# Batch 0's folds on one engine, its first DFT stage framed by zero products, its tables loaded sooner, and the order planned anew

## The chip, the cores and the metric

One core of a Trainium2 chip runs the whole program. The metric is device time in microseconds (us), the median of three runs. TensorE (PE) multiplies matrices into PSUM; VectorE (DVE) and ScalarE (ACT) work on tiles in SBUF and PSUM; GpSimd (POOL) works on SBUF and issues the indirect loads; the queue of SyncE (SP) issues all other transfers, in order. Each engine runs its own instructions in program order, and semaphores hold one engine for another.

## The reference

Eight batches of 576 tokens. Attention has 8 heads of 64 (four with a local mask of 32 tokens, four strided by 32); its output is x, 576 by 512 per batch. Then comes a mixing block: the real part of a two-dimensional Fourier transform is added to x, the sum is normalised, and two dense layers with a ReLU between them are added on top.

```python
scores = np.where(masks[None], scale * np.matmul(q, k.transpose(0, 1, 3, 2)), -1e9)
attn = softmax(scores);  x = heads_joined(np.matmul(attn, v))        # (8, 576, 512)
mixed = np.real(np.fft.fft(np.fft.fft(x, axis=1), axis=2))
u = x + mixed
un = (u - mean(u)) / np.sqrt(var(u) + 1e-6)
out = u + np.maximum(un @ w_ch1, 0.0) @ w_ch2                        # 512 -> 2048 -> 512
```

## The kernel before, in words

The work is cut into attention pairs (two heads of a batch, four pairs per batch), a Fourier transform per batch, and 18 chunks of 256 tokens for the dense layers. A chunk's first layer is its eight "ups" (line 1387, 24 matmuls each), its second layer its "downs" (line 1427). Almost all of TensorE's time goes there: W1 and W2 come as 64-bit words, are put together on ACT and DVE (lines 1215 to 1237) and split into two float16 halves (lines 1303 to 1306 for W1, 1339 to 1344 for W2), and each product takes three float16 passes. No up can run before batch 0 is through its transform and its normalisation, and no down before the halves of W2 that it reads are written.

Nothing is placed by hand. Each step is a generator that yields an `op` with an engine, an assumed duration, rooms that it takes and gives back, events that it needs, and, for some, an `alt`: a second engine with an added cost. A planner (`Order.run`) takes the ready step with the earliest start by its own clock, and among steps of that engine within a small window the one with the lowest bias. The biases, windows and added costs stand in the dictionary `P`; the program's order on every engine follows from them. While a Gram bank is open, the planner fills idle stretches of TensorE with products of zeros (`rest`, line 1272), as many as its own clock says will fit.

Batch 0 goes first, in this chain. The four pairs write their output to DRAM (lines 845 to 859). `fft_load` reads it back as `xa` in one plain load and four indirect gathers by POOL (line 897), of tokens n and 576-n. The step E adds the two, O subtracts them. Then the channels are folded, all at line 907: `cosb` and `cosd` add mirrored halves of E, `cosf` folds once more into FD, `cos2` fills FD's third group; `sin` and `sin2` do the same with O. `side(c0, c1)` forms the sums and differences of a group's two token halves: columns 0 to 129 (`side 0`) and 129 to 257 from E, 257 to 512 (`side 257`) from O. In batch 0 the planner had put E, the folds and `cos2` on DVE, and O and all three sides on POOL.

`products32` is batch 0's transform in float32. Its first stage, A, has five column groups of 65, 64, 128, 127 and 128 (0 and 1 read side 0, 2 reads side 129, 3 and 4 read side 257). A group is one product over the 33 last tokens (line 1060, 290 columns, from FD) and two over 128 tokens (line 1063, 145 columns each, from the sides); the trace shows each float32 product as two records. The tables for it, `f32a` and `f32b` (435 and 528.5 KB), are issued at line 390, and `late` makes them wait until the gathers of batch 0 have landed. ACT or DVE copies A's groups out (line 1072), then stage B multiplies by the second table (lines 1083 to 1095). B opens and closes each bank with a bf16 product of zeros:

```python
T.matmul(ps[:, 0:512], zerb, zero.to_broadcast([128, 512]), start=True, stop=False)
...
T.matmul(ps[:, 0:512], zerb, zero.to_broadcast([128, 512]), start=False, stop=True)
```

`sums` adds x (line 1099), `norm` normalises (lines 1155 to 1181), and the turned halves `uT` open the first up. Batches 3 to 7 use a float16 form of the same transform (lines 907 to 1038) with the same step names.

Of the kernel before, what the change touches and what calls it, by code (L numbers as in the profile page):

```python
# [21 lines left out]
P = dict(  # L22
    SL2=2.667, SLD2=1.764, GL0=2.7, GD=7.0, LAT=2.22, GL=3.1, t2=47.947, l0=-31.68, a0=-20, sq0=-23.456, w0a=-19.97,
    c=12.731, z=13.906, f0=-24.028, w0=-22.847, s0=-1.359, w1=3.314, s1=-5.983, p0=-26.912, p1=4.962, pn=-4.352,
    a1=-14.294, f1=-1.92, a2=0.121, f2=8.514, an=8.61, fn=-44.611, db=1.982, up=19.467, dn=25.786, ev=0.684, WS=0.271,
    WV=0.084, WA=0.048, WG=0.877, WT=0.185, SL=0.0, SLD=0.818, np=3, AL=3.136, SG=2.918, Lcl=-0.367, Lsg=0.875, LQ=0,
    LO0=12.439, LE0=13.019, Lc20=-1.501, LSD0=-13.8, al=0.0, Lfs=-1.909, Lwl=-2.741, Lul=-9.275, LO=24.795, LE=5.158,
    Lc2=-1.062, LSD=-13.902, Lsub=1.259, Lsub0=28.179, Lrt=14.582, Lu=5.511, ORD0=(3, 2, 0, 1),
    vo=([], [], [], [0, 1, 2, 3]), S0=('qk', 'qk', 'kt', 'pt'),
    S1=('uT', 'kt', 'f6', 'uT', 'kt', 'uT', 'f6', 'f6', 'kt', 'pt', 'uT', 'qk', 'u', 'f6', 'kt', 'qk'), M1=(), HB=4,  # L30
    RB=1, UB=8, VS=1, FC=15, tp=-0.006, ts=0.377, fq=-18.063, fh=-13.401, ff=-23.53, pf=5.385, Lfold=79.934, Lus=0.177,
    Lhl=1.519,
# [7 lines left out]
UB = P["UB"]  # L40
# [261 lines left out]
def body(ctx: ExitStack, tc: tile.TileContext, a, out):  # L302
# [103 lines left out]
    def att_pair(b, hp):  # L406
# [16 lines left out]
        yield op("A", 2.82 if local else 2.5, note=f"sq {nm}")  # L423
# [7 lines left out]
        yield op("V", 0.9, put="big", sets=f"vs{nm}", note=f"scales {nm}")  # L431
# [458 lines left out]
    def fft_load(b):  # L890
        yield op("S", 1.5, get="fft f6", need=" ".join(f"xd{b}_{hp}" for hp in range(4)), note=f"xa {b}")
# [11 lines left out]
    def fft_batch(b, xab=None):  # L903
# [5 lines left out]
        def side(c0, c1, nm, sd):  # L909

            cut = c1 - c0 < 200
            o = op("V", 0.5 if cut else 0.85, need=nm, sets=f"FH{c0}_{b}" if f32 else "", note=f"SD{c0}{'h' if cut else ''} {b}", alt=dict(G=(0.9 if cut else 1.43, P["LSD"] if b else P["LSD0"])))
# [20 lines left out]
        def odd():  # L933
            o = op("G", 3.45, get="f6", sets=f"O{b}", note=f"O {b}", alt=dict(V=(1.78, P["LO"] if b else P["LO0"])))
# [6 lines left out]
        o = op("V", 1.78, get="f6", note=f"E {b}", alt=dict(G=(3.45, P["LE"] if b else P["LE0"])))  # L941
# [20 lines left out]
        if f32:  # L962
            spawn(side(0, 129, "", E[:, 0:2, 0:129]))

        def cos2():
            o = op("G", 1.77, put="f6", sets=f"cos{b}", note=f"cos2 {b}", alt=dict(V=(0.6, P["Lc2"] if b else P["Lc20"])))
            yield o
            tt_(on(o), FD[:, :, 129:257], ee[:, :, 0:128], ee[:, :, 256:128:-1], ALU.subtract)

        spawn(cos2())  # L970
# [7 lines left out]
        if f32:  # L978
            spawn(side(129, 257, f"cos{b}", E[:, 0:2, 129:257]))
        else:  # L980
            spawn(side(0, 257, f"cos{b}", E[:, 0:2, 0:257]))
# [7 lines left out]
        o = op("G", 1.45, at=e - 0.6, sets=f"sin{b}", note=f"sin2 {b}", alt=dict(V=(0.6, P["Lc2"] if b else P["Lc20"])))  # L989
# [4 lines left out]
        if f32:  # L994
            yield from products32(b, FD, sds, xa, xb)
            return
# [45 lines left out]
    def products32(b, FD, sds, xa, xb):  # L1042
# [4 lines left out]
        for gs in ((0, 1), (2,), (3, 4)):  # L1047
            first, end = gs[0] == 0, gs[-1] == 4
            yield op("T", 1.4 * len(gs), get="big f6 -fft" if first else "acc" if len(gs) == 1 else "big", need=f"FH{257 if end else 0 if first else 129}_{b} f32 second",
# [5 lines left out]
            for i, g in enumerate(gs):  # L1055
# [4 lines left out]
                T.matmul(ps[0:w, 512 * i : 512 * i + 2 * NE], FD[0:33, 2, c0 : c0 + w], last[cs], start=True, stop=False)  # L1060
                for t in range(2):
                    o = ps[0:w, 512 * i + NE * t : 512 * i + NE * t + NE]
                    T.matmul(o, sd[:, t, d0 : d0 + w], ta[:, 2 * NE * cs + NE * t : 2 * NE * cs + NE * t + NE], start=False, stop=(t == 1))
# [287 lines left out]
    class Chunk:  # L1351
# [18 lines left out]
        def ups(self):  # L1370
            c = self.c
            for fp in range(8):
# [7 lines left out]
                yield op("T", 2.61, get=get.replace("h6", "f6") + " ph", put="uT" if fp == 7 else "", need=need, sets=f"up{c}" if fp == 7 else "", at=0, note=f"up {c} {fp}", slack=SLD if c else 0)  # L1380
# [27 lines left out]
        def downs(self):  # L1408
            c = self.c
            for fp in range(8):  # L1410
# [6 lines left out]
                for ss in ((0,), (1,)) if fp == 0 else ((0, 1),):  # L1417
                    yield op("T", 1.3 * len(ss), get="acc" if fp == 0 else "", put=put if ss[-1] else "", need=need, sets=f"down{c}" if fp == 7 else "", at=0, note=f"down {c} {fp}", slack=0.3)
# [470 lines left out]
```

## Time and profile before

| | |
|---|---|
| median of 3 runs | 947.85 us (946.64 to 949.21) |
| span of the profiled execution | 946.9 us |
| TensorE busy | 910.9 us, 96% of the span |
| DVE, ACT, POOL busy | 717.0, 506.2, 343.5 us |
| TensorE clock granted, mean over the span | 0.986 of full |

The profile gives the profiled execution's span and no other time for it; the span is 0.95 us under the median of the runs. A clock of 1.00 is 2.4 GHz and 0.50 is 1.2 GHz. "Busy" counts the zero products of line 1272 as work, so a busy TensorE is not always a useful one. Times inside a profile are counted from the start of its span.

### The profile page before, as it was taken

How to read it: one execution, taken by the hardware profiler on the slowest of the kernel's cores; microseconds unless marked ns; L12 is line 12 of the kernel's file. 1: busy time of each engine (PE TensorE's matmuls, PEld its weight loads, DVE VectorE, ACT ScalarE, POOL GpSimd, SP SyncE). 2: the span in 40 equal slices, each digit the busy share in tenths (PEclk: the TensorE clock that was granted, in tenths of full speed). 3: DMA queues.
4: the chain of work that ended last, by engine and by line, in shares of the span. 5: the costliest groups of instructions: out<-in, count | busy, mean ns of one | idle time of the engine just before them, and what ended most of it. 6: DMA issues, size and time to landing. Idle time of an engine off the chain costs nothing.

```text
span 946.9 us, 25320 instructions
## 1 busy us (share of the span) xinstructions
PE 910.9 (96%) x10597; PEld 668.4 (71%) x10599; DVE 717.0 (76%) x1342; ACT 506.2 (53%) x987; POOL 343.5 (36%) x315
## 2 busy tenths in 40 slices
PE   8778999999899999999999999999999999999997
PEld 6656885766666667665766677676666766689996
DVE  5988875678783896747956966697679889788675
ACT  4848874554653655643746564646423444365452
POOL 0240332245353631335325522552246256334000
PEclk9969999999999999999999999999999999999999
DMA  9788485363335635584445524625240102021100
GB/s 320 243 327 276 136 217 164 121 174 56 92 89 132 151 81 107 105 156 102 117 88 169 116 86 100 173 73 145 44 125 1 45 7 56 18 52 24 41 24 24
DMA packets 140371, 108.41 MB, mean 114 GB/s; under 512 B 108256, under 2 KB 118752, under 8 KB 140256
## 3 DMA queue, kind: packets, MB, share of 16 engines
q1 hardware_dynamic: 137696, 98.40, 38.7%
q0 software_dynamic: 2560, 8.39, 3.0%
q8 instruction: 83, 1.36, 0.6%
q14 instruction: 32, 0.26, 0.1%
HBM read 64.26 MB, written 18.89 MB: 88 GB/s over the span
## 4 chain that ended last, share of the span: by engine, by line
PE 77%; DMA 8%; DVE 7%; issue 3%; POOL 2%; ACT 2%; SPq 1%; DVEq 0%; POOLq 0%; ACTq 0%
PE acc L1427 28%; PE ph L1387 27%; PE acc L1714 5%; PE f L1571 2%; PE B L1038 2%; DMA xb<-xd,ridx 2%; DMA q<-in_w 2%; PE A L1015 1%; PE s L484 1%; DVE fold L1481 1%; PE o L515 1%; DMA W<-in_w 1%; DMA vn<-in_vl 1%; PE f_0x L1571 1%; DMA q<-in_qk 1%
## 5 line engine op out<-in xcount | busy, mean ns | idle before, releaser
L1387 PE MATMUL ph<-uT,W 128*128 128x256 f16 x2880 | 329.3, 273 | 1.2 <-DMA uT<-hb 1.2
L1387 PEld LDWEIGHTS <-W 128*128 128x128 f16 x2880 | 277.4, 98 | 42.8 <-DMA uT<-hb 1.4
L1427 PE MATMUL acc<-W,hb 128*128 128x512 f16 x1344 | 302.6, 379 | 1.5 <-DVE ub L1437 1.5
L1406 POOL TENSOR_TENSOR hb<-hf,hb 128x512 f16<-128x512 f32 x112 | 160.7, 1435 | 279.0 <-ACT hb L1404 196.5
L1427 PEld LDWEIGHTS <-hb 128*128 128x128 f16 x1344 | 129.2, 98 | 143.8 <-issue 1.7
L1403 ACT ACTIVATE hf<-ph 128x512 f32<-128x512 f32 x120 | 71.2, 593 | 180.7 <-PE ph L1387 113.1
L1404 ACT ACTIVATE hb<-ph 128x512 f16<-128x512 f32 x112 | 66.2, 591 | 0.0
L1481 DVE TENSOR_TENSOR fold<-fold,W 128x512 f32<-128x512 f32 x64 | 52.4, 847 | 0.3
L1714 PEld LDWEIGHTS <-tail 128*128 128x128 f16 x504 | 48.3, 98 | 5.3
L461 DVE SCALAR_TENSOR_TENSOR kt<-qk,sc,kt 128x576 f16<-128x576 f32 (+1 forms) x40 | 37.7, 982 | 3.3 <-ACT kt L446 3.1
L907 POOL TENSOR_TENSOR O<-xa,xb 128x1536 f32<-128x1536 f32 x8 | 33.5, 4189 | 16.0 <-DMA xb<-xd,ridx 12.4
L1161 POOL TENSOR_TENSOR rstd<-mv,negh 128x1 f32<-128x1 f32 x30 | 21.7, 730 | 44.0 <-DVE mv L1158 39.5
L1571 PEld LDWEIGHTS <-tail 128*128 128x128 f16 x576 | 34.7, 98 | 2.6 <-issue 1.4
L1658 POOL TENSOR_TENSOR hb<-hb 128x256 f32<-128x256 f32 x13 | 12.2, 950 | 65.4 <-DVE hb L1658 64.3
L1714 PE MATMUL acc<-fold,tail 128*128 128x256 f16 x288 | 35.0, 273 | 0.0
L446 ACT ACTIVATE kt<-qk,sc 128x576 f16<-128x576 f32 (+1 forms) x40 | 29.3, 784 | 10.1 <-DVE sc L402 9.0
L1140 ACT ACTIVATE pq<-B,fcm 128x128 f32<-128x128 f32 (+7 forms) x105 | 27.3, 380 | 11.5 <-PE B L1038 6.3
L1684 DVE TENSOR_TENSOR tail<-hb,tail 128x512 f16<-128x512 f32 (+1 forms) x47 | 31.8, 704 | 1.9 <-ACT tail L1681 1.5
L1681 ACT CAST tail<-hb 128x512 f16<-128x512 f32 (+1 forms) x48 | 25.6, 563 | 9.1 <-DVE hb L1658 5.5
L1179 DVE TENSOR_TENSOR unp<-un,unp 128x512 f16<-128x512 f32 x28 | 22.6, 806 | 9.1 <-ACT unp L1176 9.1
L1028 DVE SCALAR_TENSOR_TENSOR AT<-A,AT 128x290 f16<-128x290 f32 (+3 forms) x35 | 15.1, 479 | 18.8 <-ACT AT L1023 17.1
L897 POOL DMA_INDIRECT xb<-xd,ridx x24 | 26.7, 1111 | 7.3 <-issue 6.1
(313 smaller groups left out, 1550.9 us busy)
## 6 DMA issues: line engine op xcount, KB each, us to landing
qk<-in_qk SPq DMA_DIRECT2D x28, 592.0 KB
sa<-in_w SPq DMA_DIRECT2D x19, 512.0 KB
out<-ub SPq DMA_DIRECT2D x32, 256.0 KB
vn<-in_vl SPq DMA_DIRECT2D x10, 432.0 KB
W<-in_w SPq DMA_DIRECT2D x8, 512.0 KB
xd<-xo SPq DMA_DIRECT2D x16, 256.0 KB
xa<-xd SPq DMA_DIRECT2D x8, 512.0 KB
vn<-in_vs SPq DMA_DIRECT2D x10, 384.0 KB
```

The costliest lines, as they stand in the source:

```text
L446: A.activation(hi, src, AF.Copy, scale=f)
L461: V.scalar_tensor_tensor(out=lo, in0=src, scalar=f, in1=hi, op0=ALU.mult, op1=ALU.subtract)
L907: tt_ = lambda e, o, x, y, op: e.tensor_tensor(out=o, in0=x, in1=y, op=op)
L1387: T.matmul(ph[:, i, :], W1[:, 4 * (f0 // 512) + d, x, f0 % 512 : f0 % 512 + 128], self.uhl[y][:, d, :], start=(n == 0), stop=(n == 11))
L1403: A.activation(hf, ph, AF.Relu, scale=HS)
L1404: A.activation(hh, ph, AF.Relu, scale=HS)
L1406: G.tensor_tensor(out=hl, in0=hf, in1=hh, op=ALU.subtract)
L1427: T.matmul(self.acc[s], (hh, hl)[x][:, i, 128 * s : 128 * s + 128], W2[:, f, 1 - y, :], start=(f == 0 and n == 0), stop=(f == 15 and n == 2))
L1481: on(e).tensor_tensor(out=w, in0=w if x is None else x, in1=y, op=ALU.add if f else ALU.subtract)
L1571: T.matmul(dst[:, 128 * f : 128 * f + 128], w(x, i)[:, 128 * f : 128 * f + 128], u(y, i), start=opens and f == 0 and n == 0, stop=closes a ...
L1684: on(o).tensor_tensor(out=lo, in0=src, in1=hi, op=ALU.subtract)
L1714: T.matmul(dst, hop[:, x, j, 128 * i : 128 * i + 128], w(y, i), start=bank not in opened, stop=q == 3 and z in (6, 5, 3, 4) and i == 1 and ...
```

## The change

In batch 0 the steps E, O, `cos2`, `sin2` and the three sides lose their second engine and go to DVE, and their order there is fixed: E, `cosb`, `cosd`, `cosf`, side 0, `cos2`, then O, `sin`, `sin2`, side 257, with side 129 a step of its own as soon as `cos2` is done. Each group of stage A is opened and closed by a bf16 product of zeros over its 290 columns, and the product over the 33 last tokens comes after the two others. The tables `f32a` and `f32b` no longer wait for the gathers; in the plan they follow `xa`'s plain load. Most of `P` has new values, and some assumed durations are raised by some per cent, so the order on every engine is a new one from start to end.

```diff
-    a0=-20, sq0=-23.456, w0a=-19.97, c=12.731, z=13.906, f0=-24.028, w0=-22.847, s0=-1.359, w1=3.314, s1=-5.983, ...
+    a0=3.023, sq0=-19.729, w0a=-28.451, c=34.197, z=3.51, f0=-35.267, w0=-19.94, s0=-9.387, w1=14.964, s1=-13.897, ...
-    LAT=2.22, ORD0=(3, 2, 0, 1), S0=('qk', 'qk', 'kt', 'pt'), ...
+    LAT=52.805, ORD0=(3, 2, 1, 0), S0=('uT', 'qk', 'qk', 'pt'), ...
     def consts():
-        yield op("S", 1.9, n=2, need="xb0", sets="f32", note="f32")
+        yield op("S", 2.9, n=2, need="xa0", sets="f32", note="f32")
-            late(nc.sync.dma_start(tab32[n], a[n]))
+            nc.sync.dma_start(tab32[n], a[n])
     def side(c0, c1, nm, sd):
-            o = op("V", ..., alt=dict(G=(0.9 if cut else 1.43, P["LSD"] if b else P["LSD0"])))
+            o = op("V", ..., alt=None if f32 else dict(G=(0.9 if cut else 1.43, P["LSD"])))
     def odd():
-            o = op("G", 3.45, ..., alt=dict(V=(1.78, P["LO"] if b else P["LO0"])))
+            o = op("V", 1.78, ...) if f32 else op("G", 3.45, ..., alt=dict(V=(1.78, P["LO"])))
-        spawn(odd())
+        if not f32:
+            spawn(odd())
...
-        if f32:
-            spawn(side(0, 129, "", E[:, 0:2, 0:129]))
+        if f32:
+            spawn(products32(b, FD, sds, xa, xb))
+            yield from side(0, 129, "", E[:, 0:2, 0:129])
+            yield from cos2()
+            spawn(side(129, 257, "", E[:, 0:2, 129:257]))
+            yield from odd()
     def products32(b, FD, sds, xa, xb):
-            yield op("T", 1.4 * len(gs), ...)
+            yield op("T", 1.6 * len(gs), ...)
-                T.matmul(ps[0:w, 512 * i : 512 * i + 2 * NE], FD[0:33, 2, c0 : c0 + w], last[cs], start=True, stop=False)
+                both = ps[0:w, 512 * i : 512 * i + 2 * NE]
+                T.matmul(both, zerb[:, 0:w], zero.to_broadcast([128, 2 * NE]), start=True, stop=False)
                 for t in range(2):
-                    T.matmul(o, sd[:, t, d0 : d0 + w], ta[...], start=False, stop=(t == 1))
+                    T.matmul(both[:, NE * t : NE * t + NE], sd[:, t, d0 : d0 + w], ta[...], start=False, stop=False)
+                T.matmul(both, FD[0:33, 2, c0 : c0 + w], last[cs], start=False, stop=False)
+                T.matmul(both, zerb[:, 0:w], zero.to_broadcast([128, 2 * NE]), start=False, stop=True)
```

In the dictionary, `a0` is the bias of batch 0's attention, `w0a` that of W1's first three quarters, `w0` and `s0` of its last quarter, `w1` and `s1` of W2's loads and splits, `f0` of batch 0's transform, `c` of the tables. Outside batch 0 the steps keep both engines, with other added costs; the assumed up goes from 2.61 to 2.64 and the down from 1.3 to 1.312.

## Rows read from the trace of the kernel before

**Rows 1.** The page: busy time, share of the span and instructions by engine.
```profile
PE 910.9 (96%) x10597; PEld 668.4 (71%) x10599; DVE 717.0 (76%) x1342; ACT 506.2 (53%) x987; POOL 343.5 (36%) x315
```
**Rows 2.** Windows: stretch, length, busy PE PEld DVE ACT POOL, clock, DMA share, GB/s.
```profile
0.00:95.00 95.00, 74.97 (x1053) 59.46 (x1056) 75.81 (x140) 59.04 (x75) 19.00 (x19) 0.87 0.86 292
95.00:143.00 48.00, 47.34 (x703) 40.74 (x701) 38.16 (x78) 39.02 (x57) 18.80 (x17) 1.00 0.65 180
210.00:252.00 42.00, 39.31 (x487) 28.88 (x485) 34.58 (x58) 22.37 (x44) 20.35 (x18) 1.00 0.32 79
40.00:50.00 10.00, 8.28 (x138) 7.83 (x138) 8.33 (x13) 4.54 (x5) 5.45 (x4) 0.99 0.52 159
53.00:54.00 1.00, 0.00 (x0) 0.00 (x0) 1.00 (x1) 0.00 (x0) 1.00 (x1) 0.92 0.88 288
54.00:69.00 15.00, 11.67 (x28) 5.80 (x29) 13.96 (x22) 8.62 (x16) 5.88 (x7) 0.50 1.00 386
75.00:83.00 8.00, 7.91 (x47) 4.95 (x51) 7.18 (x20) 7.37 (x12) 0.57 (x1) 1.00 0.99 357
```
**Rows 3.** Windows of line 1272 alone: length, busy PE and PEld, clock, DMA.
```profile
95.00:143.00 48.00, 0.00 (x0) 0.00 (x0) 1.00 0.65 180
0.00:947.00 947.00, 26.32 (x370) 24.59 (x370) 0.99 0.42 114
```
**Rows 4.** Timeline of DVE and POOL, batch 0's folds (start, length, instruction, idle before).
```profile
50.05 1.76 DVE L907 TENSOR_TENSOR E<-xa,xb 128x1536 f32<-128x1536 f32 x1 [1.08 <-DMA xb<-xd,ridx]
50.09 5.00 POOL L907 TENSOR_TENSOR O<-xa,xb 128x1536 f32<-128x1536 f32 x1 [2.75 <-DMA xb<-xd,ridx]
51.85 4.05 DVE L907 TENSOR_TENSOR tmp<-E 128x765 f32<-128x765 f32 x1
56.00 0.56 DVE L907 TENSOR_TENSOR tmp<-tmp 128x384 f32<-128x384 f32 x1
56.67 0.63 DVE L907 TENSOR_TENSOR FD<-tmp 128x192 f32<-128x192 f32 x2
57.21 0.95 DVE L907 TENSOR_TENSOR E<-O 128x765 f32<-128x765 f32 x1
57.44 1.76 POOL L907 TENSOR_TENSOR E<-FD 128x129 f32<-128x129 f32 x2 [2.35 <-DVE FD L907]
```
**Rows 5.** Timeline of TensorE, the first stage and what follows.
```profile
48.83 2.84 PE L1272 MATMUL gram<-oneb,zero 128*128 128x128 bf16 x48
57.13 1.20 PE L1060 MATMUL A<-f32a,FD 33*65 33x290 f32 x2 [5.45 <-DVE FD L907]
64.78 1.33 PE L1060 MATMUL A<-f32b,FD 33*127 33x290 f32 x2
67.31 1.33 PE L1060 MATMUL A<-f32b,FD 33*128 33x290 f32 x2
69.69 1.92 PE L1264 MATMUL gram<-W 128*128 128x128 bf16 x16
73.97 0.55 PE L1083 MATMUL B<-zero 128*128 128x512 bf16 x1
76.88 0.38 PE L1083 MATMUL B<-zero 128*128 128x512 bf16 x1
77.09 0.33 PE L1089 MATMUL B<-f32b,AT 65*128 65x65 f32 x2
```
**Rows 6.** Timeline of TensorE, first up and first long run of downs.
```profile
92.32 8.03 PE L1387 MATMUL ph<-uT,W 128*128 128x256 f16 x72 [1.21 <-DMA uT<-hb]
142.78 3.41 PE L1427 MATMUL acc<-W,h 128*128 128x512 f16 x15
```
**Rows 7.** Timeline of the SP queue (start, issue time).
```profile
39.62 0.36 SPq L893 DMA_DIRECT2D xa<-xd  x1
49.85 0.36 SPq L390 DMA_DIRECT2D f32a<-in_f32a  x1
130.24 0.70 SPq L1344 DMA_DIRECT2D W<-fs  x1
```

More of the change, by code (lines that the diff above doesn't have):

```diff
@@ L890, in fft_load @@
     def fft_load(b):
-        yield op("S", 1.5, get="fft f6", need=" ".join(f"xd{b}_{hp}" for hp in range(4)), note=f"xa {b}")
+        yield op("S", 1.5, get="fft f6", need=" ".join(f"xd{b}_{hp}" for hp in range(4)), sets=f"xa{b}", note=f"xa {b}")
         xa = f6(f"xa{b}").rearrange("p (t c) -> p t c", t=3)
@@ L911, in side @@
             cut = c1 - c0 < 200
[L912 removed]
+            o = op("V", 0.5 if cut else 0.85, need=nm, sets=f"FH{c0}_{b}" if f32 else "", note=f"SD{c0}{'h' if cut else ''} {b}", alt=None if f32 else dict(G=(0.9 if cut else 1.43, P["LSD"])))
             yield o
@@ L976, in fft_batch @@
             FH = hl.FH = f6(f"FH{b}").bitcast(F16).rearrange("p (i t c) -> p i t c", i=2, t=3)
-        if f32:
-            spawn(side(129, 257, f"cos{b}", E[:, 0:2, 129:257]))
-        else:
+        if not f32:
             spawn(side(0, 257, f"cos{b}", E[:, 0:2, 0:257]))
@@ L988, in fft_batch @@
         A.copy(FD[:, :, 511:512], oo[:, :, 128:129])
-        o = op("G", 1.45, at=e - 0.6, sets=f"sin{b}", note=f"sin2 {b}", alt=dict(V=(0.6, P["Lc2"] if b else P["Lc20"])))
+        o = op("V", 0.6, at=e - 0.6, sets=f"sin{b}", note=f"sin2 {b}", alt=None if f32 else dict(G=(1.45, -P["Lc2"])))
         yield o
@@ L1048, in products32 @@
             first, end = gs[0] == 0, gs[-1] == 4
-            yield op("T", 1.4 * len(gs), get="big f6 -fft" if first else "acc" if len(gs) == 1 else "big", need=f"FH{257 if end else 0 if first else 129}_{b} f32 second",
+            yield op("T", 1.6 * len(gs), get="big f6 -fft" if first else "acc" if len(gs) == 1 else "big", need=f"FH{257 if end else 0 if first else 129}_{b} f32 second",
                      put="f6 f6 f6" if end else "", note=f"A{gs[0]} {b}")
@@ L1379, in ups @@
                     need += f" up{c - 1}"
-                yield op("T", 2.61, get=get.replace("h6", "f6") + " ph", put="uT" if fp == 7 else "", need=need, sets=f"up{c}" if fp == 7 else "", at=0, note=f"up {c} {fp}", slack=SLD if c else 0)
+                yield op("T", 2.64, get=get.replace("h6", "f6") + " ph", put="uT" if fp == 7 else "", need=need, sets=f"up{c}" if fp == 7 else "", at=0, note=f"up {c} {fp}", slack=SLD if c else 0)
                 ph = pph.tile([128, 512], F32, tag="ph", name=f"ph{c}_{fp}").rearrange("p (i t) -> p i t", i=2)
@@ L1417, in downs @@
                 for ss in ((0,), (1,)) if fp == 0 else ((0, 1),):
-                    yield op("T", 1.3 * len(ss), get="acc" if fp == 0 else "", put=put if ss[-1] else "", need=need, sets=f"down{c}" if fp == 7 else "", at=0, note=f"down {c} {fp}", slack=0.3)
+                    yield op("T", 1.312 * len(ss), get="acc" if fp == 0 else "", put=put if ss[-1] else "", need=need, sets=f"down{c}" if fp == 7 else "", at=0, note=f"down {c} {fp}", slack=0.3)
                     if ss[0] == 0:
```

36 lines of the change are left out of this document (17 added, 19 removed).

## The prediction

> **What bounds the kernel now.** I read the page first. TensorE is busy 910.9 of 946.9 us [rows 1], so 36.0 us are left, and the only question is where TensorE waits and where its work is not needed. The windows say where: of the 36.0 us, 95.0 - 74.97 = 20.0 lie in the first 95 us [rows 2]. The windows of line 1272 alone add that 26.3 us of the busy time are products of zeros, none of them between 95 and 143 us [rows 3]. So the head wastes more than the other 850 us together. From the first up at 92.32 us [rows 6] it turns round: 95 to 143 has 0.66 us idle and no filling [rows 2, 3]. TensorE is the bound from there, and when the first up starts decides the end as long as nothing behind it runs dry.
>
> What holds the first up is batch 0's chain. In the timeline of DVE and POOL the reader is to see a fold of 765 elements that takes 4.05 us, while the same shape takes 0.95 us some microseconds later [rows 4]. The slow one starts at 51.85 and ends at 55.90, and POOL's O runs from 50.09 to 55.09: DVE finishes 0.81 us after POOL lets go. Then TensorE: its zero products end at 51.67, it idles 5.45 us, and stage A's groups follow at 2.53 us each (64.78 to 67.31) [rows 5]. The clock is the reason for 2.53: it falls late in the window 53 to 54 (mean 0.92), in that idle stretch, and is 0.50 from 54 to 69; stage B then runs at 1.00 [rows 2]. So 54 to 69 are at 1.2 GHz, with batch 0 as TensorE's only work.
>
> **The change part by part.** All times on the clock of the profiled span.
>
> *Folds on DVE.* With no O on POOL the 765-element fold costs 0.95 and ends at 51.85 + 0.95 = 52.80. From its end to the end of FD the old rows have 57.30 - 55.90 = 1.40 [rows 4], so FD is there at 54.20, not 57.30. The sides are not on DVE in this trace. Nearest: 192 elements in 0.32 (two in 0.63) and 384 in 0.56; on POOL 129 elements take 0.88 (two in 1.76) [rows 4]. So 129 elements lie between nothing and 0.32 or, from above, 0.88; I take 0.30, near the DVE row; 255 elements lie between 0.32 and 0.56, I take 0.44. The chain: side 0 two times 0.30, to 54.80; cos2 as 384 elements, 0.56, to 55.36; side 129, to 55.96; O as E, 1.76, to 57.72; sin 0.95 + 0.56, to 59.23; sin2 0.56, to 59.79; side 257 two times 0.44, to 60.67; with the 0.04 between instructions, 61.0. DVE gains 0.6 + 0.6 + 1.76 + 0.88 = 3.8 us of work and loses the 3.1 of waiting: 0.7 net, in a stretch where it did little but wait on these folds. POOL loses its O and sides, and nothing else wanted it then.
>
> *The first stage.* TensorE can start at 54.80, not 57.13. Whether the clock is up is the main choice. Before, it fell some two microseconds into the idle stretch. Zero products that open a bank need no data, so one more piece of work stands in the stretch, but if the filling still ends at 51.67 TensorE idles 3 us before side 0. Stage B is float32 too, has a zero product at either end of each bank, and stays at 1.00 through eight microseconds [rows 2, 5]; the first stage has none and stays at 0.50 though busy. I take it that the framed stage is at full clock. A group is then 2.53 / 2 = 1.27. A frame of 512 columns costs 0.21 from its start to the next product's (76.88 to 77.09) [rows 5]; 290 columns cost between 290/512 of that, 0.12, and 0.38, the whole length of that product; I take 0.20, near the spacing, so a group is 1.67. Three groups end at 59.8, the last two wait for side 257 at 61.0 and end at 64.3. Before: 67.31 + 2.53 = 69.84. That is 5.5 earlier. ACT's copies and the order of the 33-token product cost nothing: the copies lie beside the Gram and score products that TensorE had between the stages.
>
> Here the Trainium skill ("TensorE: Matmul & The Clock Gate", "Part 1: The HAM clock gate") speaks against the frames: the clock is throttled by default and activity of the array releases it. By that rule the busy stage A would have come back to full clock by itself; the row of 54 to 69 at 0.50 disagrees, and beside B's row it leaves the frames as the difference. By the page the frames buy nothing and cost 10 x 0.20 = 2 us; by the rows they decide 5.5 us.
>
> *What stands between the stages.* From 69.84 to 73.97 TensorE did 20 Gram products and a score block at half clock [rows 5]: 4.1 us, 2.05 at full. So stage B starts 5.5 + 2.05 = 7.6 earlier. B is at full clock already; from its start to the first up the trace has 92.32 - 73.97 = 18.35 us on DVE, POOL and a transposing load, and I leave that as it is.
>
> *Tables.* SP issues xa at 39.62 and the tables at 49.85, behind the gathers [rows 7]. At 40 us their 963.5 KB (987 kB) meet the gathers. At the 386 GB/s of the full stretch 54 to 69 they take 2.6 us; from 40 to 50 the DMA engines are 48% idle, 4.8 us [rows 2]. So the cost is between nothing and 2.6; I take 0.5 for gathers that queue behind them. SP's later issues keep their place: csin and the weights still wait for the gathers, and they find the engines free of the tables.
>
> *Order anew.* The new biases change every stretch. W1's pieces now go ahead of batch 0's attention where both are ready, and W2's go further back (w1 from 3.3 to 15.0). TensorE reached its first long run of downs at 142.78, while the first halves of W2 were written at 130.24 [rows 6, 7]: a slack of 12.5 us, more than the head can gain. Behind that I see one place that is not tied to the head: 210 to 252 has 42.0 - 39.31 = 2.7 us idle with DVE at 82% [rows 2]. If that chain stays where it is, TensorE waits longer there by what it came sooner. Bounds: nothing is given back, or all of it; I take 1.6.
>
> *Sum.* -7.6 + 0.5 + 1.6 = -5.5: the span goes from 946.9 to 941.4. The page gives no time but the span, which lies 0.95 under the median of the runs; with that, 942.3 us.
>
> **The rivals.**
>
> *The clock stays low in stage A.* It falls in the shorter idle stretch too, and the frames do not lift it again. For it: it fell early in the idle stretch before, and 12 us of busy TensorE did not lift it. Against: B's row. A group is then 2.53 + 4 x 0.20 = 3.3 and five end at 54.8 + 16.7 = 71.5, 1.6 later than before. With nothing gained behind it: 949.4 us; with frames at 0.12, 948 or less.
>
> *The head's gain is given back.* Stage B starts early, but the first run of downs or the stretch at 210 to 252 is set by chains on DVE and the DMA engines (both near full from 75 to 83 us, 7.18 of 8 and 0.99 [rows 2]). For it: W2's later place in the plan. Against: the 12.5 us of slack. The time: 946 to 949.
>
> *The new order starves TensorE further on.* Place: the stretches where the next batch's attention and transform must be ready, as 210 to 252, DVE at 82%. Price: 2.7 us each. It decides from (5.5 + 2.8) / 2.7, some three more such stalls, on the side of slower; four make 947.85 - 5.5 + 10.8 = 953.2. For it: the whole order is replaced, and the plan's own clock was off in this kernel: it let the filling end 5.45 us before stage A could start [rows 5]. Against: outside batch 0 no step changes its cost or loses an engine that it used.
>
> *The frames do not do what they are for but the folds do:* covered by the first rival's price when the clock falls, and by the forecast's when it does not.
>
> **How the numbers follow.** Under 0.3%, 2.8 us, a measurement of this kernel can't be told from no change: faster is below 945.0, slower above 950.7. The forecast has 0.56, and its own range is 938 to 945.5, from side costs, frames, the gather and what is given back; 0.53 of it is faster. The low clock has 0.12, all of it no change. The gain given back has 0.13, of which 0.03 is faster. Starving has 0.19, of which 0.17 is slower. Together: faster 0.56, no change 0.27, slower 0.17. The range 935.5 to 951 leaves out some 0.06 below, an order that also takes the old stalls away, and some 0.13 above.
>
> **What would show it.** Right: the 765-element fold in about 0.95 us; O and all sides on DVE; side 0 done some 5 us after E starts; stage A's groups at 1.5 to 1.8 us with a granted clock of 1.00; the tables issued next to xa; the first up before 87 us and no filling or idle time to speak of from there to 140. Wrong: a granted clock of 0.50 in stage A, gathers that land over 2 us later after xa's issue, TensorE idle in front of the first downs, or more idle time between 200 and 800 us than the 36.0 - 20.0 = 16.0 us now behind 95 us, part of which is the end itself.

## The result, and the profile after

The changed kernel is slower: 958.75 us (955.20 to 965.55, 4 runs) beside 948.53 for the kernel before on the same chip, ratio 1.011, 95% interval 1.0063 to 1.0158. On a second chip it took 959.38 (1.0105, 1.0083 to 1.0127), on a third 970.84 (1.0219, 1.0197 to 1.0241). The prediction was 942.3, faster, with 0.17 on slower. The profiled execution is the shortest of the first four (span 953.4, its time 955.20).

The page, engines [rows 1]: POOL is relieved of its folds. TensorE is busy 4.8 us longer than before and idle 1.7 us longer (37.7 for 36.0), which together are the 6.5 us by which the span grew.

```profile
PE 915.7 (96%) x10585; PEld 670.1 (70%) x10585; DVE 713.8 (75%) x1358; ACT 509.0 (53%) x989; POOL 313.5 (33%) x297
```

Windows of the stretches of [rows 2] (columns as there); the third line is the whole low-clock stretch around stage A, 17.0 us at 0.50 (1.2 GHz).

```profile
0.00:95.00 95.00, 72.54 (x1020) 56.09 (x1020) 68.92 (x137) 57.27 (x73) 9.04 (x12) 0.89 0.86 284
95.00:143.00 48.00, 45.32 (x622) 39.93 (x623) 39.09 (x82) 38.33 (x58) 16.96 (x13) 1.00 0.54 154
55.70:72.70 17.00, 16.28 (x57) 9.82 (x57) 10.82 (x22) 6.59 (x13) 0.00 (x0) 0.50 0.76 288
210.00:252.00 42.00, 39.96 (x458) 27.61 (x457) 37.59 (x62) 22.67 (x45) 26.49 (x19) 0.98 0.52 137
```

From 0 to 95 us TensorE now idles 22.5 us instead of 20.0, from 95 to 143 us 2.7 instead of 0.7; behind 143 us it idles less, 12.6 instead of 15.3. The filling alone [rows 3], line 1276 here, is 25.5 us instead of 26.3:

```profile
95.00:143.00 48.00, 0.00 (x0) 0.00 (x0) 1.00 0.54 154
0.00:953.00 953.00, 25.49 (x346) 23.50 (x346) 0.98 0.43 114
```

DVE's folds in its timeline [rows 4]. The 765-element fold takes 0.95 as forecast, and side 0 (`E<-FD` of 129) ends 4.75 us after E's start, as forecast.

```profile
51.82 1.76 DVE L906 TENSOR_TENSOR E<-xa,xb 128x1536 f32<-128x1536 f32 x1 [1.15 <-DMA xb<-xd,ridx]
53.61 0.95 DVE L906 TENSOR_TENSOR tmp<-E 128x765 f32<-128x765 f32 x1
56.07 0.50 DVE L906 TENSOR_TENSOR E<-FD 128x129 f32<-128x129 f32 x2
56.95 1.75 DVE L906 TENSOR_TENSOR O<-xa,xb 128x1536 f32<-128x1536 f32 x1
61.13 0.76 DVE L906 TENSOR_TENSOR O<-FD 128x255 f32<-128x255 f32 x2
```

TensorE's timeline, stage A to stage B [rows 5], and the first up and downs [rows 6]. A group is 2.90 us from frame to frame (64.81 to 67.71), not 1.67, and there is no score block between A and B any more.

```profile
52.85 0.29 PE L1063 MATMUL A<-zero 128*65 128x290 bf16 x1
56.42 1.23 PE L1065 MATMUL A<-f32a,E 128*65 128x145 f32 x4 [3.29 <-DVE E L906]
64.81 0.45 PE L1063 MATMUL A<-zero 128*127 128x290 bf16 x1
67.71 0.45 PE L1063 MATMUL A<-zero 128*128 128x290 bf16 x1
70.31 0.42 PE L1067 MATMUL A<-zero 128*128 128x290 bf16 x1
72.13 0.63 PE L1087 MATMUL B<-zero 128*128 128x512 bf16 x1
95.41 1.80 PE L1391 MATMUL ph<-uT,W 128*128 128x256 f16 x15 [1.71 <-issue]
142.88 2.75 PE L1431 MATMUL acc<-W,h 128*128 128x512 f16 x12
```

142.88 is the first of all downs here. In the kernel before the first downs came at 136.01 (the run at 142.78 in [rows 6] is the next one):

```profile
136.01 1.46 PE L1427 MATMUL acc<-W,h 128*128 128x512 f16 x6
```

So the changed kernel is 3.1 us behind at the first up and 6.9 at the first downs. From there to the end it takes 810.5 us, the kernel before 810.9: in these two profiles the whole loss stands ahead of the first downs.

The queue of SP [rows 7]: the tables go next to xa, xa itself 1.7 us later than before; the first halves of W2 (130.24 before) go 6.6 us later.

```profile
41.34 0.37 SPq L892 DMA_DIRECT2D xa<-xd  x1
41.75 0.47 SPq L389 DMA_DIRECT2D f32a<-in_f32a  x1
82.71 0.42 SPq L614 DMA_DIRECT2D vlx<-in_v  x1
136.85 0.70 SPq L1348 DMA_DIRECT2D W<-fs  x1
```

The chain of waits up to the first up (start, length, what). In the kernel before, this stretch of the chain ran through batch 0's own normalisation; here it runs through a load of batch 1.

```profile
81.46 0.86 PE s L579 x44
82.33 0.33 SPq L610
82.71 7.00 DMA vlx<-in_v
89.80 1.26 ACT jk L621 x2
91.06 1.24 ACT sa L1235
92.32 0.70 DVE W L1241
93.07 0.63 PE gram L1268 x8
93.70 1.71 issue
95.41 4.64 PE ph L1391 x41
```

Read backwards: the first up stands in TensorE's order behind a Gram product of W2; that needs a conversion on ACT, which stands behind the squares of batch 1's values (`vlx`, line 621); their load stands behind a `qk` load, which waits for the room that batch 1's first score block gives back; and that block (81.46) now stands behind stage B. Before, it stood between A and B, and the load (there line 615) went 8.7 us sooner:

```profile
71.41 0.74 PE L573 MATMUL s<-mstr,ident 128*128 128x324 bf16 x2
74.04 1.74 SPq L615 DMA_DIRECT2D vlx<-in_v  x1
```

### The profile page after: what moved, and what is told of

The parts are those of the page before. It is cut to its first block, busy times and chain, and to the rows that moved or that the text cites. A ratio compares the mean times of both kernels' runs of the same rounds, so it can differ in the third digit from the quotient of the medians.

```text
span 953.4 us, 25279 instructions
## 1 busy us (share of the span) xinstructions
PE 915.7 (96%) x10585; PEld 670.1 (70%) x10585; DVE 713.8 (75%) x1358; ACT 509.0 (53%) x989; POOL 313.5 (33%) x297
## 4 chain that ended last, share of the span: by engine, by line
PE 79%; DMA 8%; DVE 7%; issue 2%; ACT 2%; SPq 1%; POOL 1%; DVEq 0%; POOLq 0%; ACTq 0%
PE acc L1431 28%; PE ph L1391 28%; PE acc L1718 5%; DMA vlx<-in_v 3%; PE f L1575 2%; PE B L1040 2%; DMA xb<-xd,ridx 2%; PE A L1017 2%; PE s L483 1%; DMA W<-in_w 1%; PE o L514 1%; PE f_0x L1575 1%; DMA xd<-xo 1%; DVE kt L460 1%; PE f_2x L1575 1%
## 5 line engine op out<-in xcount | busy, mean ns | idle before, releaser
L1410 POOL TENSOR_TENSOR hb<-hf,hb 128x512 f16<-128x512 f32 x112 | 151.7, 1355 | 282.3 <-ACT hb L1408 198.3
L906 POOL TENSOR_TENSOR O<-xa,xb 128x1536 f32<-128x1536 f32 x7 | 26.9, 3836 | 21.0 <-PE acc L1431 14.0
L1688 DVE TENSOR_TENSOR tail<-hb,tail 128x512 f16<-128x512 f32 (+1 forms) x42 | 27.2, 674 | 6.6 <-ACT tail L1685 6.5
L1136 DVE TENSOR_TENSOR rt<-pq 128x257 f32<-128x257 f32 (+1 forms) x42 | 17.6, 460 | 17.1 <-ACT pq L1144 9.2
```

The source lines that it names most:

```text
L1410: G.tensor_tensor(out=hl, in0=hf, in1=hh, op=ALU.subtract)
L1688: on(o).tensor_tensor(out=lo, in0=src, in1=hi, op=ALU.subtract)
```

## The experiments

Each kernel was timed beside the kernel before; only kernels of one chip are compared in microseconds. Times of stages are from one profile each. The profiled execution is not the median one: a_fill's took 955.38 us, a_plan29_2's, the longest of its twelve, 950.83. "A" is stage A's first float32 product to its last, "B to up" from stage B's start to the first up.

| kernel | chip | us | ratio (95%) | A | B to up | first downs |
|---|---|---|---|---|---|---|
| before | | | | 12.77 | 18.34 | 136.01 |
| changed | first | 958.75 | 1.011 (1.0063 to 1.0158) | 13.96 | 23.28 | 142.88 |
| a_fill | 4 | 949.79 | 1.0005 (0.9976 to 1.0034) | 12.54 | 27.37 | 149.52 |
| b_fill | 4 | 946.96 | 0.9975 (0.9959 to 0.999) | 10.99 | 16.89 | 135.17 |
| a_noframe | 4 | 953.42 | 1.0036 (1.0016 to 1.0055) | 12.25 | 23.39 | 140.15 |
| a_plan29 | 4 | 948.84 | 0.9977 (0.9955 to 0.9999) | 13.97 | 20.02 | 136.50 |
| a_dense | 3 | 950.25 | 1.0008 (0.9986 to 1.003) | 10.68 | 23.41 | 139.43 |
| a_plan_nf | 3 | 949.20 | 0.999 (0.9972 to 1.0008) | 12.25 | 18.04 | 136.17 |
| a_oldp | 3 | 967.81 | 1.0178 (1.015 to 1.0207) | 13.44 | 23.66 | 156.39 |
| b_newp | 3 | 1001.03 | 1.0526 (1.0497 to 1.0554) | 11.98 | 17.42 | 140.73 |
| a_swap | 11 | 959.77 | 1.0107 (1.0076 to 1.0138) | 12.75 | 27.80 | 146.28 |
| a_late | 11 | 958.53 | 1.0089 (1.0054 to 1.0124) | 13.96 | 25.78 | 145.64 |
| c_dense | 11 | 997.82 | 1.0493 (1.0459 to 1.0527) | 10.67 | 20.44 | 136.53 |
| b_dense | 11 | 950.25 | 0.9994 (0.9976 to 1.0012) | 10.76 | 19.32 | 136.73 |
| a_scores | 2 | 966.72 | 1.0185 (1.016 to 1.0209) | 13.96 | 19.43 | 141.46 |
| a_both | 2 | 964.79 | 1.0147 (1.0123 to 1.0172) | 13.74 | 20.12 | 141.91 |
| a_again | 2 | 970.84 | 1.0219 (1.0197 to 1.0241) | 13.96 | 26.40 | 148.25 |
| c_plan29_fill | 2 | 957.33 | 1.0079 (1.0055 to 1.0103) | 8.30 | 20.87 | 136.25 |
| a_again2 | 6 | 959.38 | 1.0105 (1.0083 to 1.0127) | 13.97 | 27.72 | 147.13 |
| a_plan29_2 | 6 | 946.26 | 0.9967 (0.9947 to 0.9987) | 13.96 | 18.98 | 137.13 |

### The clock in stage A

a_fill is the changed kernel, b_fill the kernel before, each with zero products into the open Gram bank ahead of the first group; a_noframe is the changed kernel without frames, its small product first.

```diff
 a_fill, b_fill
             if first:
+                rest(66)        # b_fill: rest(100)
 a_noframe
-                T.matmul(both, zerb[:, 0:w], zero..., start=True, stop=False)
+                T.matmul(ps[0:w, 512 * i : 512 * i + 2 * NE], FD[0:33, 2, c0 : c0 + w], last[cs], start=True, stop=False)
...
-                T.matmul(both, zerb[:, 0:w], zero..., start=False, stop=True)
```

> The changed kernel with 66 more filling products of zeros on TensorE just ahead of stage A's first group, so that TensorE does not idle while the folds run. Order otherwise the same. Theory 1 (the clock): the clock falls in the idle stretch ahead of stage A, stage A runs at half clock, and the order, planned for a fast stage A, makes ACT wait for it; with the filling the granted clock is 1.00 through stage A, a group takes 1.4 to 1.7 us, stage A ends near 64 us, ACT's waits for stage A shrink to under 2 us in sum, the first up starts at 86 to 89 us, and the time is 942 to 949. Theory 2 (the order): the new order of W2 and of batch 1's loads is late whatever stage A does; stage A is faster but the time stays at 954 to 960.

> The kernel before with 100 more filling products of zeros ahead of stage A's first group; its stage A has no frames. If the idle stretch alone drops the clock and float32 products hold it: clock 1.00 through stage A, groups of about 1.27 us, time 940 to 945. If float32 products without frames do not hold the clock: it falls a few us into stage A, the last groups take 2.5 us, time 945 to 949.

> The changed kernel without the ten zero products that open and close stage A's groups, and with the product over the last tokens first again, as before the change. Theory 1 (clock): the clock still falls ahead of stage A, groups of 2.5 us instead of 2.9, the stage ends some 2 us sooner, time equal or up to 3 us under the changed kernel's. Theory 3 (the frames are what costs): back to 946 to 950.

Both fillings kept the clock at 1.00 into stage A, and in both profiles it fell inside the stage: in a_fill at 60.3 us, 1.8 us into the stage, which had begun behind a wait of 2.73 us; in b_fill at 64.5 us, 5.0 us into a stage that had begun without a wait, but in the second of two waits for POOL's side 129 (0.79 and 0.35 us). Windows of a_fill, ahead of the fall and behind it, and its first product, then b_fill behind its fall and the product ahead of it (columns as in [rows 2]):

```profile
52.00:60.00 8.00, 5.27 (x74) 4.26 (x72) 5.76 (x9) 0.60 (x3) 0.00 (x0) 1.00 0.74 224
60.50:71.00 10.50, 10.50 (x30) 5.76 (x29) 7.77 (x18) 4.68 (x9) 0.00 (x0) 0.50 0.77 286
58.49 0.71 PE L1066 MATMUL A<-f32a,E 128*65 128x145 f32 x4 [2.73 <-DVE E L906]
```

```profile
64.60:70.50 5.90, 5.90 (x17) 3.72 (x18) 5.43 (x11) 4.50 (x9) 0.00 (x0) 0.50 0.93 328
63.71 0.52 PE L1064 MATMUL A<-f32a,E 128*128 128x145 f32 x2 [0.79 <-POOL E L907]
```

So the long idle stretch ahead of the stage is not needed for the fall: b_fill had none. And once the clock was at 0.50, busy float32 products did not bring it back, with frames (a_fill) or without (b_fill). Whether short waits or the float32 products themselves lowered it, these two don't show. a_fill's runs spread from 943.70 to 957.51, the shortest with a mean clock of 0.990 and 0.991, the longest with 0.981. b_fill is where its second case had it, 946.96. a_noframe has the low clock for as long (17.1 us, as in the changed kernel's profile), and its stage is 1.7 us shorter: the frames bought nothing and cost 0.34 a group. Its time, 1.0036 of the kernel before, met neither theory: it lies under the changed kernel's 1.011 and 1.0105 by more than those 1.7 us, and why is open.

a_dense and b_dense put six zero products into a group, one pair behind each float32 product, with the fillings of a_fill and b_fill.

```diff
                 for t in range(2):
                     T.matmul(both[:, NE * t : NE * t + NE], sd[:, t, d0 : d0 + w], ta[...], start=False, stop=False)
+                    for _ in range(2):
+                        T.matmul(both, zerb[:, 0:w], zero..., start=False, stop=False)
                 T.matmul(both, FD[0:33, 2, c0 : c0 + w], last[cs], start=False, stop=False)
-                T.matmul(both, zerb[:, 0:w], zero..., start=False, stop=True)
+                for k in range(2):
+                    T.matmul(both, zerb[:, 0:w], zero..., start=False, stop=(k == 1))
```

> The changed kernel, same order of instructions, with 66 zero products of 128 columns ahead of the first group of stage A and six bf16 zero products of 290 columns in each group instead of two (after each float32 product as well as at the ends). Theory 1 (what holds the clock is bf16 work; the float32 products count for little, and two frames a group are too few): the granted clock stays at 1.00 through the whole stage in nearly every execution, a group takes 1.27 + 6 x 0.2 = 2.5 us or less, first up before 89 us in the profile, and times stand together near the low group of the kernel with filling alone, 943 to 949 us, without a group at 952 to 958. Theory 2 (the chip lowers the clock in this stretch whatever TensorE does, for instance because of the filling before it): it falls again in stage A, a group then takes 2.53 + 6 x 0.2 to 0.4 = 3.7 to 4.9 us, and the time is 955 us or more.

> The kernel before with its own order, 100 zero products of 128 columns ahead of stage A and six bf16 zero products in each group; folds, tables and plan as before. If bf16 work in the groups is what holds the clock: granted clock 1.00 through stage A here too, a group 2.2 us instead of 2.53, stage A's end about 3 us earlier than 69.84 (five groups, and the Gram products behind it at full clock), and 943 to 947 us if the old order passes half of it on; 948 to 950 if it gives it all back before the first downs. If the clock falls in spite of them: groups of 3.5 us and more, 952 us or above.

a_dense's windows of stage A and stage B, both at full clock:

```profile
56.00:67.00 11.00, 10.81 (x64) 6.86 (x65) 8.73 (x18) 4.70 (x9) 0.00 (x0) 1.00 0.83 320
67.00:76.30 9.30, 9.30 (x63) 6.43 (x62) 7.66 (x21) 8.72 (x14) 0.00 (x0) 1.00 0.98 378
```

That is what theory 1 says of the clock, and all twelve runs of a_dense have a mean clock of 0.989 to 0.995, where a_fill's have 0.981 to 0.991. But the profile of a_dense waits only 1.09 us ahead of the stage and b_dense's not at all, so fewer waits are a rival that isn't ruled out; and c_plan29_fill, below, had two zero products a group, a wait of 1.12 us ahead, and 1.00 through the stage. A group then takes 2.14 us (10.68 / 5), where 2.45 did at half clock without frames (a_noframe) and 1.27 at full clock without frames (b_fill, 60.90 to 62.17): the six zero products take back 0.87 of the 1.18 us. The time is not the 943 to 947 that I had hoped for: 950.25 in both, no change. In b_dense the stage is 2.0 us shorter than in the kernel before and starts 3.2 us later (60.37), since 100 zero products run past the data. In a_dense stage B starts at 67.91, 6.1 us earlier than before, and the first up only 1.0 us earlier (91.32): B to up is 23.41 instead of 18.34. The lead is gone there, at full clock up to 90 us: TensorE idles 5.0 us from 76.3 to 90, and the last of its waits there, 2.94 us for W on DVE (line 1245), stands ahead of the last Gram products before the first up.

### Which order

a_plan29 changes one number of the changed kernel: the duration that the planner assumes for a group. The instructions are the same but for the filling and one step that goes from ACT to DVE; their order is not. a_plan_nf does so without frames, c_dense with a_dense's groups.

```diff
-            yield op("T", 1.6 * len(gs), ...)
+            yield op("T", 2.9 * len(gs), ...)      # a_plan_nf: 2.5, c_dense: 2.2
```

> The changed kernel with the planner told that a group of stage A takes 2.9 us instead of 1.6: the same instructions in another order, ACT's work on the weights now ahead of stage A's copies. Theory 1, its second half (an order planned for a fast stage A costs when the stage is slow): the clock still falls to 0.50, but ACT no longer waits for stage A, batch 1's loads are issued 5 to 8 us sooner, the first up starts at 90 to 93 us, time 946 to 951. Theory 2: 954 to 960 again.

> The changed kernel without the frames, planned with 2.5 us for each group of stage A instead of 1.6. If the two costs found so far add up (frames about 5 us of the changed kernel's time, the plan about 10 us): the plan with the frames gave 948.8, so without them 944 to 946 us. If they are one cost (the frames only hurt because the planner does not know of the long stage): 947 to 950 us, as with the frames.

> The changed kernel with filling ahead of stage A and six bf16 zero products in each group (which held the clock at 1.00), and the planner now told 2.2 us for a group, which is what it then takes, instead of 1.6. Theory 1 (what a clock at 1.00 gained in the head was given back ahead of the first downs because the order behind stage A is planned for other times): with a plan that fits, the first downs come before 134 us and the time is 942 to 947 us. Theory 2 (the head's gain is given back whatever the order, since W2's conversions on ScalarE and VectorE set the first downs): the first up near 89 us, the first downs again at 135 to 137, and the time 947 to 951 us.

a_plan29 gave the whole loss back with the clock still low (0.50 from 55 to past 78 us, longer than in the changed kernel's profile). a_plan_nf (949.20) gave it back too, and adds nothing to it: its first up comes at 88.82, 3.5 us ahead of the kernel before, and its first downs at 136.17, 0.2 behind. That is the second rival of the prediction, the lead given back ahead of the first downs; what holds them there was not tried. Since the chips differ, it was run again beside the unchanged kernel.

> The changed kernel as it is, beside the same kernel planned with 2.9 us for a group on one chip. 957 to 961 us as on two chips so far, or 968 to 972 as on the third.

> The changed kernel planned with 2.9 us instead of 1.6 for a group of stage A, once more. Theory 1 (the order is the loss): 8 to 12 us under the changed kernel beside it, whichever of its two times that has. Theory 2 (the gap to the earlier run was the chip's): less than 4 us under it.

959.38 and 946.26: 13.1 us on one chip by that number alone, and the second is faster than the kernel before (0.9967, 0.9947 to 0.9987; 0.9977, 0.9955 to 0.9999 on the other chip). It is the fastest version of the study that holds on two chips. A part of the 13.1 may be the clock, since its mean is 0.977 to 0.980 in the one and 0.981 to 0.988 in the other; but at nearly the same clock, 0.980 and 0.981, the runs are 956.58 and 956.62 beside 946.03 to 950.83. The two profiles below are the shortest run of the one and the longest of the other, 5.7 us apart, so they show where the orders differ and not what each difference is worth. TensorE's timeline, a_again2 and then a_plan29_2: the score block behind the last part of stage B, or in front of its first.

```profile
81.18 0.38 PE L1087 MATMUL B<-zero 128*128 128x512 bf16 x1
84.27 0.46 PE L572 MATMUL s<-mstr,ident 128*128 128x324 bf16 x2
98.60 1.65 PE L1391 MATMUL ph<-uT,W 128*128 128x256 f16 x7 [1.73 <-issue]
```

```profile
73.53 0.74 PE L572 MATMUL s<-mstr,ident 128*128 128x324 bf16 x2
75.67 0.61 PE L1087 MATMUL B<-zero 128*128 128x512 bf16 x1
94.65 2.79 PE L1391 MATMUL ph<-uT,W 128*128 128x256 f16 x24 [2.13 <-DMA uT<-hb]
```

The queues of SP of the two, same order; the load that the first up hangs on goes 9.8 us earlier, and the first up waits for its own `uT` again.

```profile
85.98 0.43 SPq L614 DMA_DIRECT2D vlx<-in_v  x1
```

```profile
76.14 0.43 SPq L614 DMA_DIRECT2D vlx<-in_v  x1
```

c_dense was told what its groups take, and lost 47 us. Its first up (88.75) and first downs (136.53) are good; the loss lies behind 400 us, where TensorE idles 11.8 us from 400 to 500 and 18.6 from 800 to 900 (2.6 and 1.2 in the kernel before); why was not tried. So a true duration is no guarantee: each value makes another order of some 2,500 steps, and some are far worse. Whether 2.9 won because it is the true duration or as a lucky draw is therefore open. a_oldp and b_newp exchange the dictionaries: the changed code with the old dictionary, and the old code with the new one.

```diff
-P = dict(... new values ...)
+P = dict(... old values ...)      # a_oldp; b_newp the other way round
```

> The changed kernel's steps with the dictionary P of the kernel before: all edits of the structure, planned with the old biases. Theory 1 (the loss is the order that was planned anew around a stage A of 1.6 us a group, with ACT's first conversions of W2 behind the copies of stage A): the old biases hold the copies and conversions in another order, so ACT does not wait for stage A ahead of the conversions and the time is within 4 us of the kernel before, 945 to 953 us. Theory 2 (the loss is in the structure itself: folds all on DVE, frames, tables early): as slow as the changed kernel, 955 us or more, with stage A at half clock in both cases.

> The kernel before with the new dictionary P alone: no frames, the tables still behind the gathers, O and the sides free to go to POOL. Theory 1 (the new order carries the loss): 952 us or more, with the first conversions of W2 on ACT behind stage A's copies and batch 1's loads after 66 us. Theory 2 (the structure carries it): 946 to 951 us.

Taken by themselves they contradict each other: a_oldp is as theory 2 has it (the structure), b_newp as theory 1 (the order), and b_newp loses far more, 51 us, than the change did. So they don't divide the loss. What they show is that either dictionary does badly with the code that it was not fitted to. (b_newp kept 1.4 us a group; its stage A starts only at 71.86.)

### Which place in the order

To test one place without a new plan, three kernels issue the changed kernel's steps from a written list, its own order with the moves below. c1 and sg are the conversions of W1's pieces 12 to 15 (lines 1225 and 1235), AT the copies of stage A's groups.

```diff
 a_swap, ScalarE
-AT0, c1 12, AT1, AT2, c1 13, sg 12, c1 14, c1 15, AT3, c1 of W2, AT4, sg 15, sg of W2
+c1 12, c1 13, c1 14, c1 15, AT0, AT1, sg 12, AT2, c1 of W2, sg 15, sg of W2, AT3, AT4
 a_scores, TensorE
-B0, B1, B2, gram 14, gram 15, scores 1_3
+scores 1_3, B0, B1, B2, gram 14, gram 15
 a_scores, SyncE
-four loads of W2, load 1_1 (qk), load 1_1 (vlx)
+load 1_1 (qk), load 1_1 (vlx), four loads of W2
```

a_scores also has that block's maxima and differences on DVE ahead of `sums`; a_both is a_swap and a_scores together.

> The changed kernel with every instruction and the order of TensorE, VectorE, GpSimd and the queue of SyncE as they are; on ScalarE alone nine steps stand differently: the first conversions of W1's pieces 12 to 15 ahead of stage A's first copy, and stage A's later copies behind the conversions that no longer need to wait for them. Theory 1 (the convoy: ScalarE's conversions stand behind copies that wait for a slow stage A, the loads of batch 1 wait for the rooms of those pieces): ScalarE idles less than 2 us for stage A, batch 1's first load is issued by 65 us instead of 68.6, the first up comes 2 us or more earlier than 95.4 and the first downs before 140, and the time is 950 to 955 us. Theory 2 (every replanned order differs by some microseconds by chance, and the one planned with 2.9 us was a better draw): 957 to 961 us, as the changed kernel's 958.75.

> The changed kernel in its own order but for one step and what goes with it: batch 1's first score block (pair 1_3) stands in front of stage B on TensorE instead of behind it, its two maxima and differences on VectorE in front of the u sums, and the two loads of pair 1_1, which take the room that the block gives back, four loads earlier on SyncE's queue. Theory 1 (this place holds the first up): vlx of batch 1 is issued before 78 us instead of 82.7, the first up comes 2 to 4 us earlier than in the changed kernel's profile (95.4) at the same granted clock, and the time is 951 to 956 us. Theory 2 (a plan is a draw, no single place carries it): 957 to 961 us.

> The edits of a_scores and of a_swap together: batch 1's first score block in front of stage B, and ScalarE's conversions ahead of the copies that wait for stage A. If the two places are one chain (ScalarE lets the loads go at 65 us, and the block in front of stage B lets the next loads follow): vlx issued by 75 us, first up by 93 us, first downs by 139, and 947 to 953 us, near the 948.8 of the plan with 2.9 us. If the order's price is spread over many places: 955 us or more.

> The changed kernel as it is, for its time beside the others on this chip and a second profile: 956 to 961 us. If its run-to-run differences are those of the clock, a slower execution shows more half-clock time after stage A (through stage B, as in a_late) and an order of work that is otherwise the same.

a_swap was my theory, and it fell. ScalarE's waits for stage A are gone and batch 1's first load goes at 65.17, but `vlx` goes at 85.03, for the score block still stands behind stage B, and the time is that of a_late on its chip (959.77, 958.53). a_scores is 4.1 us under a_again, the unchanged order on its chip, with runs of 965.66 to 969.86 and 968.95 to 971.51 (3.3 us between the means), a_both 6.1 (960.53 to 967.71). a_again's queue of SP, then a_scores':

```profile
86.30 0.42 SPq L614 DMA_DIRECT2D vlx<-in_v  x1
```

```profile
75.43 0.34 SPq L614 DMA_DIRECT2D vlx<-in_v  x1
```

B to up goes from 26.40 to 19.43 (stage B starts 2.3 us later, behind the block), the first up from 99.41 to 94.70, the first downs from 148.25 to 141.46. So the place is real and is worth some 4 us, of which the clock may have a share: in a_scores' profile it is back at 1.00 some 3 us sooner. With ScalarE's steps, which give nothing alone, it is 6, where the whole order was worth 13 on another chip. What the other 7 hang on is open: between the first up and the first downs the orders planned with 1.6 take 47 to 49 us and a_plan29's 42.5, in part other work moved ahead, in part idle TensorE (1.8 us from 100 to 137 in a_again2, none in a_plan29_2).

### The tables, and filling with the better order

```diff
 a_late
-            nc.sync.dma_start(tab32[n], a[n])
+            late(nc.sync.dma_start(tab32[n], a[n]))
```

> The changed kernel, same order of instructions on every engine, with the tables f32a and f32b held back behind the gathers again. If loading them early cost next to nothing, as the two profiles say (10.22 and 10.26 us from xa's issue to the last gather's landing): 957 to 960 us, and the last gather lands within 0.5 us of 51.6. If they push the gathers back by the 0.5 us of the forecast or more: 955 to 958 us and an earlier last gather. If their early place is what gains time in the head: stage A waits for them and the time is above 961 us.

958.53, 1.0089 of the kernel before: early or late, the tables cost and give nothing that these runs can tell. From xa's issue to E's start there are 10.48 us in the changed kernel and 10.73 in a_late, 10.43 before.

c_plan29_fill is a_plan29 with `rest(66)`.

> The changed kernel planned with 2.9 us for a group, and 66 zero products of 128 columns ahead of stage A. If filling and order add up: 943 to 947 us, faster than the kernel before. If the filling only moves the fall of the clock into the stage and its return into the first ups, as in a_fill's slower executions: 947 to 951 us.

It missed both: 957.33, on the chip where the changed kernel takes 970.84. That is 13.5 us under it, about what the order alone gave on another chip (13.1); a_plan29 was not run on this chip, so what the filling added can't be told. Its stage A is what I had forecast for the change, five framed groups at full clock, 8.30 us or 1.66 a group. The clock fell behind the stage, at 66.9 us, after TensorE had idled 1.6 of the 2.9 us since the stage's end; stage B, framed as ever, began at 0.50 and was at 0.50 until 77 us:

```profile
55.00:64.00 9.00, 7.96 (x38) 4.48 (x38) 8.66 (x19) 4.11 (x8) 0.00 (x0) 1.00 0.99 373
67.00:77.00 10.00, 8.00 (x65) 6.04 (x67) 6.48 (x16) 6.86 (x11) 0.00 (x0) 0.50 1.02 382
71.42 0.59 PE L1088 MATMUL B<-zero 128*128 128x512 bf16 x1 [1.59 <-ACT AT L1077]
```

## Why the prediction was wrong

By the profile the span came out at 953.4 instead of 941.4. The 12.0 us lie in three terms of the sum.

*"I take it that the framed stage is at full clock"*, the choice on which the forecast rested. It failed: 0.50 from 55.70 to 72.70 us. Stage B started at 72.13, where the sum had 66.87 with its 0.5 for the gather: 5.3 us. (About 1 of these is a later start, 56.42 for 55.30, because this execution issued xa late.) The size of a framed group was right (1.66 in c_plan29_fill for 1.67), the clock was not. I read stage B's 1.00 as the work of its frames. But in the kernel before B began at 0.50 and was back at 1.00 within its first microsecond (the window 74 to 75 has 0.84), behind some 4 us of Gram products and a score block; a single frame had gone by. In a_again2 B's frames did nothing of the kind: 10.1 us of busy, framed float32 work at 0.50.

```profile
70.90:81.00 10.10, 10.10 (x30) 7.48 (x29) 3.81 (x10) 7.19 (x11) 0.00 (x0) 0.50 0.73 256
```

Nor did A's frames bring the clock back in the changed kernel or in a_fill. With six zero products a group it stayed at 1.00 through the stage (a_dense), and these take back three quarters of what the clock gives. The Trainium skill ("TensorE: Matmul & The Clock Gate", "Part 1: The HAM clock gate") has activity of the array release the throttle; with float32 products the traces disagree: a_fill's TensorE was busy 10.50 of 10.50 us and stayed at 0.50. The prediction had drawn from that rule of the Trainium skill that the frames buy nothing: they bought nothing, but the stage did not come back by itself either. The first rival on record, 949.4, had this clock and 3.3 us a group; it left the order out.

*"From its start to the first up the trace has 92.32 - 73.97 = 18.35 us ..., and I leave that as it is."* It took 23.28: 4.9 us. I had counted the score block between A and B as work that a full clock halves, and did not ask where the new order puts it. It went behind stage B, and the loads, squares, conversions and Gram products behind it came in front of the first up. a_scores shows that place and what goes with it alone; a_dense, in the same order, shows a lead at stage B of 6.1 us that is down to 1.0 at the first up although the clock held. So the forecast would probably have been short with the clock right as well: a_dense, which has four more zero products in each group, took 950.25, and a_fill's four runs with a mean clock of 0.990 or more took 943.70 to 948.23, on average 3.5 us under the kernel before on their chip, where the forecast had 5.5.

*The order, 1.6 us given back.* From the first up to the end it is 854.6 before and 858.0 after: 3.4, a miss of 1.8. I had looked at 210 to 252, which gained (2.0 us idle for 2.7); the loss came at once, 95 to 143, where I had seen a slack of 12.5 us. That slack was misread: it is counted to the downs at 142.78, and the first ones stood at 136.01, 5.8 us behind the first halves of W2 at 130.24. In the changed kernel it is 142.88 and 136.85, 6.0 us. Whether the downs hang on these halves is not shown: TensorE does not wait right in front of them.

The profiled execution is the shortest of its four; the others are up to 10.4 us longer, with mean clocks down to 0.975 from 0.984. In a_again2's profile the low clock lasts through most of stage B, to 81 us, and B to up is 27.72.

Right were the folds (4.75 us from E to side 0, O and all sides on DVE), and the tables at no cost (I had taken 0.5). xa is issued 1.7 us later than before in this profile, 0.5 in a_again2's (40.13) and 0.3 in a_late's (39.96), so I don't count it as a cost of the change. The third rival, a starving order, was on the right side, with the wrong place and price: I looked behind 200 us, where the idle time fell, and TensorE's idle time grew by 1.7 us in all.

## What to carry to other kernels

When a change replaces an order that a planner wrote, compare the new order step by step in the stretch that holds the first dependent work: find what each queue now has ahead of it, above all loads that wait for a room. A duration in the plan is a choice of order: one number (1.6 for a group that took 2.9) was worth 13 us here, but another true one (2.2 in c_dense) lost 47, so an order has to be timed and not trusted. And filling that keeps a clock up is work too: six zero products a group took back 0.87 of the 1.18 us that the clock gave.

## What the runs showed of the hardware

With six bf16 zero products in each group of float32 products the clock was at 1.00 through stage A in all three profiles (a_dense; b_dense, from 60 to 71 us; c_dense). With two it was so in c_plan29_fill, and it fell after 1.8 us of a_fill's stage, which had waited longer ahead of it (2.73 us, 1.12 in c_plan29_fill). Once it was at 0.50, float32 products did not raise it: busy 14.20 of 14.20 us in the changed kernel (56.5 to 70.7), 10.50 of 10.50 in a_fill, 10.10 of 10.10 in a_again2's stage B. Zero products and waits changed together in these runs, so which of them keeps the clock up is open.

The new order also depends on the chip, the old one much less: the changed kernel took 959.38 on one chip and 970.84 on another, where the kernel before took 948.75 and 950.77. In a_again, on the second of these, TensorE waits inside a batch's score block for nothing that the profile shows; a_late's profile has no such wait. Waits of TensorE from 600 to 660 us (line, waited for, us in total, times, longest):

```profile
PE s L483 <- issue: 2.7, 4, 1.2
PE o L521 <- DMA pT<-pbt: 1.3, 1, 1.3
```

What causes it was not tried.
